# First block of an RWKV and two-expert-layer kernel: routing columns in column halves, three small steps on other engines, another written order

## The chip, the cores and the metric

One core of one Trainium2 chip runs the whole program in one launch. The metric is the device time in microseconds of that core, the median of several runs. The kernel before takes 879.41 us (median of 3 runs, 879.02 to 879.43).

## The reference, cut to what matters

```python
# stage 1: attention with decay, B=4, H=8, S=768, D=48
for t in range(S):
    y[:, :, t] = r_t @ (state + (u * k_t) v_t^T)
    state = w_t * state + k_t v_t^T
x = y as rows [3072, 384]
# stage 2: gated layer, d_ff = 1536
xn = x / sqrt(mean(x * x) + 1e-6) * rms_g
x = (silu(xn @ w_gate) * (xn @ w_val)) @ w_out
# stage 3: 8 experts, top 1, d_ff = 1024
logits = x @ moe2_w_gate ; e = argmax ; gate_w = softmax(logits)[e]
out[rows of e] = gate_w * sigmoid(x @ w_output_gate[:, e]) * (relu(x @ w1[e]) @ w2[e])
```

The logits and the output gate of stage 3 need x only through two small matrices of 384 x 8 each. The kernel folds them into stage 2: the rows of w_out are lengthened from 384 to 400 columns by w_out times those 16 columns. These 16 are the routing columns.

## The kernel before, in words

Stage 2 handles the 3072 rows in 8 blocks of 384 (j = 0 to 7). Within a block, f runs over the 12 parts of d_ff, 128 each. For every f, l1 multiplies x by the gate and value weights (18 matmuls of L170, three for each product: high by high, high by low, low by high), ScalarE takes the silu and VectorE the product h (L546 in the first block). Two f later, l2 adds h times the 400 columns into three accumulators (L560 in the first block). While block j goes through l1 and l2, the attention of the three 128-row tiles of block j+1 is laid between them.

Attention of a tile is a generator (attention, L350 to L501) with nine pieces, each ended by a yield: a scan for kq (L370); the decay and kq product, and k times r on GpSimd (L383, L385); a second scan and rq (L390, L393); a transpose of kq on TensorE (L414), the four small products that give the gains g (L420), g out of PSUM (L424) and the bonus, v times g, on GpSimd (L404); the scores (L437) and their mask on VectorE (L441); the sum with v (L456), y on VectorE (L460), its square on ScalarE (L464), and on GpSimd the mean (L465) and the power -1/2 (L466); the state (L472, L482); the scaling of y (L486); the transposes of y (L490) and x as a high and a low part (xh L494, xl L497). Tiles 0 to 5 are "bare": their g comes from TensorE as told; later tiles take it from another load.

The weights of stage 2 arrive in HBM as 64-bit floats and are decoded on the chip while the first block runs: 18 parts, of which 12 are gate and value weights and 6 are pairs of w_out rows. A part (decode, L101 to L136) goes through five stages: load; low word on ScalarE (L116) and shift on VectorE (L117); merge on VectorE (L121) and sum on GpSimd (L125); high part on ScalarE (L133); low part on VectorE (L135). A step of decoding (decode_step, L772) takes one stage or two of each of several parts; l1 and l2 call it at every second slot. When a pair of w_out rows is decoded, route_columns makes the routing columns of each of its two parts f: three transposes (L512), one copy to SBUF (L515), three matmuls of 128 columns of weights by 16 (L519), and one copy into the lengthened rows (L520).

Everything is in one written order (a manual schedule): each engine takes its instructions in the order in which the program issues them. Before the first l1 that order is START_SEQ: 0, 1 and 2 advance the attention of that tile by one piece, 9 is one decode_step, a negative number -n is n matmuls on constants that feed nothing (warm, L344), and 99 is columns_of (L201), which turns u and rms_g. In the first block OFFS and TGAP say at which slot each piece of tiles 3 to 5 comes. A slot is one call from l1 or l2, 36 in the block.

```python
for d in START: ...            # 99, -n, 9, or a tile
def slot():
    plan.step()
    if plan.slot % 2:
        decode_step()
```

Of the kernel before, what the change touches and what calls it, by code (L numbers as in the profile page):

```python
# [22 lines left out]
def kernel(  # L23
# [15 lines left out]
    ROUTE_AT=(0, 3),  # L39
    OFFS=((0, 0, 6.7, 7.5, 8.8, 10.5, 11.4, 11.5, 12.7), (0, 1.6, 3.2, 4.8, 6.4, 8, 9.6, 11.6, 13.8)),  # L40
    TGAP=(8.9, 9.0),
    START_SEQ=(-11, 0, 0, 0, -4, -4, -6, -1, 99, 0, 1, 0, 1, -4, 9, 0, 1, 1, 2, -4, 0, 0, 1, 9, 2, 0, 1, -4, 2, -6, 1, 9, 2, 1, 2, -4, 1, 2, 9, -2, 2, 2, 9, -6, 2, 9),
):
# [307 lines left out]
    def attention(c, i, xh, xl, col):  # L351
# [31 lines left out]
        nc.vector.tensor_tensor(out=kq, in0=kT, in1=kq, op=ALU.mult)  # L383
        if bare:
            nc.gpsimd.tensor_tensor(out=kT, in0=kT, in1=rT, op=ALU.mult)  # L385
        yield
# [5 lines left out]
        )  # L392
        nc.vector.tensor_tensor(out=rq, in0=rT, in1=rq, op=ALU.mult)  # L393
        if i != NSET and not bare:
            load_tile(i + NSET + (i < NSET))
# [15 lines left out]
        if not last:  # L411
# [4 lines left out]
            nc.scalar.activation(out=kt, in_=kt_ps, func=AF.Copy)  # L416
        if bare:
            g_ps = bank("m", 3, [P, H])
            for p in range(NPR):
                nc.tensor.matmul(  # L420
                    g_ps[:, 2 * p:2 * p + 2], kT[0:64 + D, p], c["u2"][0:64 + D, p], start=True,
                    stop=True,
                )
            nc.scalar.activation(out=g, in_=g_ps, func=AF.Copy)  # L424
            bonus()
            if i != NSET:
                load_tile(i + NSET + (i < NSET))
        if ch:
# [10 lines left out]
        for q in range(2):  # L439
            m = p2.tile([P, NPR, P], F32, tag="am", name="am")  # L440
            nc.vector.tensor_tensor(  # L441
                out=m, in0=ab[q], in1=c["tri"].unsqueeze(1).to_broadcast([P, NPR, P]), op=ALU.mult
            )
            am.append(m)
        yield
        yp = bank("m", 3, [P, H, D])
# [60 lines left out]

    def route_columns(f, tf):

        o = bank("m", 3, [P, KD, P])  # L510
        for kk in range(KD):
            nc.tensor.transpose(o[:, kk], tf[:, kk * P:(kk + 1) * P], c["ident"])  # L512

        wt = p3.tile([P, DM], F32, tag="hl", name="wt").rearrange("p (c f) -> p c f", c=KD)
        nc.scalar.activation(out=wt, in_=o, func=AF.Copy)  # L515
        yield
        o = bank("m", 3, [P, 2 * E])
        for kk in range(KD):
            nc.tensor.matmul(o, wt[:, kk], c["wr"][:, kk], start=kk == 0, stop=kk == KD - 1)  # L519
        nc.scalar.activation(out=whole_w[f // 2][:, f % 2, DM:WIDTH], in_=o, func=AF.Copy)  # L520
        yield

    def split_wo(k):

        for f in (2 * k, 2 * k + 1):
            if f in routed:
                exhaust(routed.pop(f))
        wo[k] = ring.tile([P, 2, 2, WIDTH], FR, tag="big", bufs=6, name="wo")
# [147 lines left out]
    with tc.manual_schedule():  # L676
# [34 lines left out]
        for f in range(KF):  # L711
# [8 lines left out]
            if f % 2:  # L720
# [7 lines left out]

                def more(tf, f=f):
                    for i in range(2):  # L730
                        routed[f - 1 + i] = route_columns(f - 1 + i, tf[:, i])

# [9 lines left out]
        def routed_step():  # L742

            n = done_w[0]
            for f in sorted(routed):
                if f not in plan_r:
                    plan_r[f] = {n + f % 2, n + f % 2 + 2}
                if n in plan_r[f] and next(routed[f], 1):
                    del routed[f]
            for f in [f for f in routed if max(plan_r[f]) < n]:  # L750
                exhaust(routed.pop(f))

# [107 lines left out]
        for j in range(NB):  # L860
# [8 lines left out]
            if j + 1 < NB:  # L869
                nxs = new_x(j + 1)  # L870
                for a in range(sizes[j + 1]):
                    plan.add(
                        attention(c, starts[j + 1] + a, nxs[0], nxs[1], a * P),
                        a * TGAP[j > 0], OFFS[j > 0],
                    )

            def slot():
                plan.step()

                if plan.slot % 2:  # L880
                    decode_step()
# [3 lines left out]
            for f in range(KF + 2):  # L885
# [453 lines left out]
```

## Time and profile before

| | |
|---|---|
| median of 3 runs | 879.41 us |
| the profiled execution | 878.36 us |
| its span, first to last instruction | 876.7 us |
| mean granted TensorE clock | 0.976 |
| TensorE busy | 850.6 us (97%) |
| VectorE busy | 516.8 us (59%) |
| ScalarE busy | 310.0 us (35%) |
| GpSimd busy | 210.4 us (24%) |
| first matmul of l1 in the first block | 47.43 us |
| end of the first block | about 145.9 us |

The profile comes from one execution, whose own time is 1.66 us more than its span and 1.05 us less than the median. Times in a row are microseconds from the start of the span. PE is TensorE, PEld its weight loads, DVE VectorE, ACT ScalarE, POOL GpSimd. A clock of 1.00 is 2.4 GHz, 0.50 is 1.2 GHz. The profile counts two records for each matmul of fp32 operands, so x6 for L519 are three matmuls.

### The profile page before, as it was taken

What the parts mean: (1) busy time and instruction counts of PE and PEld (TensorE: products, weight loads), DVE (VectorE), ACT (ScalarE), POOL (GpSimd) and SP (SyncE); (2) the same over time, 40 slices, a digit from 0 to 9 for tenths busy, and PEclk for the clock granted to TensorE, in tenths of its full rate; (3) what the DMA queues carried; (4) which work ended last, traced back from release to release, by engine and by line L of the source; (5) the groups of instructions that cost most, each with busy time, mean ns of one, the idle gap of its engine ahead of it and who ended that gap; (6) DMA issues with size and microseconds to landing.
All of it is one profiled execution on the core that took longest, in us unless ns stands there. A gap on an engine that the chain in (4) does not pass through costs nothing. (4 is left out here: it accounts for less than half of the span.)

```text
span 876.7 us, 15834 instructions
## 1 busy us (share of the span) xinstructions
PE 850.6 (97%) x6175; PEld 798.5 (91%) x6175; DVE 516.8 (59%) x1027; ACT 310.0 (35%) x653; POOL 210.4 (24%) x282
## 2 busy tenths in 40 slices
PE   7889999999999999999999999999999999999995
PEld 5677878999999999999999999999999999999994
DVE  7788946763764565565376366343646565565641
ACT  4455334322223222322322223223435434443430
POOL 6555522222321122032132132010021022122111
PEclk8669999999999999999999999999999999999998
DMA  8654421762222222131023020012255444435510
GB/s 234 200 166 133 138 89 48 192 186 81 83 55 55 65 65 64 30 99 55 10 88 81 24 82 19 2 40 82 71 184 159 141 157 148 153 121 177 175 42 23
DMA packets 63728, 87.98 MB, mean 100 GB/s; under 512 B 5538, under 2 KB 55220, under 8 KB 63652
## 3 DMA queue, kind: packets, MB, share of 16 engines
q1 hardware_dynamic: 60014, 77.36, 30.1%
q0 software_dynamic: 3312, 9.56, 2.9%
q8 instruction: 49, 0.80, 0.4%
q14 instruction: 27, 0.22, 0.1%
q10 hardware_dynamic: 326, 0.03, 0.0%
HBM read 70.71 MB, written 16.58 MB: 100 GB/s over the span
## 5 line engine op out<-in xcount | busy, mean ns | idle before, releaser
L170 PE MATMUL a<-xh,gv 128*128 128x384 f32 x1152 | 324.7, 347 | 1.6 <-ACT xh L494 1.6
L170 PEld LDWEIGHTS a<-xh,gv 128*128 128x128 f32 x1152 | 212.7, 190 | 5.3 <-ACT xh L494 1.7
L170 PE MATMUL a<-xl,gv 128*128 128x384 f32 x576 | 195.3, 339 | 0.2 <-DVE xl L497 0.2
L170 PEld LDWEIGHTS a<-xl,gv 128*128 128x128 f32 x576 | 109.5, 190 | 1.2 <-DVE xl L497 0.6
L549 DVE TENSOR_TENSOR sil<-a,sil 128x384 f32<-128x384 f32 x84 | 46.7, 555 | 107.1 <-PE a L170 106.0
L542 ACT ACTIVATE sil<-a 128x384 f32<-128x384 f32 x96 | 47.1, 491 | 175.5 <-PE a L170 170.1
L170 PE MATMUL a<-xh,w1s 128*128 128x272 f32 (+7 forms) x384 | 106.1, 337 | 0.4 <-DVE hl L1003 0.4
L551 ACT ACTIVATE hh<-sil 128x384 fp32r<-128x384 f32 x84 | 44.1, 524 | 144.1 <-DVE sil L549 142.4
L571 PE MATMUL l<-wo,hh 128*128 128x400 f32 x252 | 88.5, 351 | 0.0
L572 PE MATMUL l<-wo,hh 128*128 128x400 f32 x252 | 86.5, 343 | 0.0
L573 PE MATMUL l<-wo,hl 128*128 128x400 f32 x252 | 86.2, 342 | 0.0
L246 POOL DMA_INDIRECT out_dram<-row,iu x30 | 35.4, 1179 | 189.3 <-DVE row L1014 146.2
L1003 DVE SCALAR_TENSOR_TENSOR hl<-a,hh 128x256 fp32r<-128x256 f32 (+8 forms) x72 | 38.6, 539 | 68.3 <-ACT hh L1002 68.3
L170 PEld LDWEIGHTS a<-xh,w1s 128*128 128x128 f32 x384 | 69.8, 188 | 2.0 <-DVE hl L1003 0.7
L1002 ACT ACTIVATE hh<-a 128x256 fp32r<-128x256 f32 (+8 forms) x72 | 34.5, 479 | 93.9 <-PE a L170 93.3
L170 PE MATMUL l<-hh,rows 128*128 128x272 f32 (+4 forms) x240 | 67.5, 346 | 0.0
L554 DVE TENSOR_TENSOR hl<-sil,hh 128x384 fp32r<-128x384 f32 x84 | 46.7, 556 | 31.9 <-ACT hh L551 31.9
L170 PE MATMUL a<-xl,w1s 128*128 128x272 f32 (+7 forms) x192 | 64.5, 336 | 0.1
L404 POOL TENSOR_TENSOR y<-vt,g 128x384 f32<-128x384 f32 x23 | 21.0, 914 | 167.0 <-issue 67.9
L571 PEld LDWEIGHTS l<-wo,hh 128*128 128x128 f32 x252 | 47.2, 187 | 1.0
L572 PEld LDWEIGHTS l<-wo,hh 128*128 128x128 f32 x252 | 47.4, 188 | 0.0
L573 PEld LDWEIGHTS l<-wo,hl 128*128 128x128 f32 x252 | 47.2, 187 | 0.0
(250 smaller groups left out, 1453.3 us busy)
## 6 DMA issues: line engine op xcount, KB each, us to landing
raw<-in_moe_w_dram SPq DMA_DIRECT2D x64, 384.0 KB, 3.3
set<-in_feat_dram SPq DMA_DIRECT2D x46, 192.0 KB, 3.6
rk<-in_rkv_dram SPq DMA_DIRECT2D x18, 384.0 KB, 4.1
scr<-zrow SPq DMA_DIRECT2D x8, 788.0 KB, 6.2
set<-in_feat_dram SPq DMA_DIRECT2D x46, 96.0 KB, 2.5
vt<-in_rkv_dram SPq DMA_DIRECT2D x23, 192.0 KB, 2.8
raw<-in_moe_w_gate_dram SPq DMA_DIRECT2D x8, 384.0 KB, 4.6
raw<-in_moe_w_val_dram SPq DMA_DIRECT2D x8, 384.0 KB, 4.0
```

The costliest lines, as they stand in the source:

```text
L170: nc.tensor.matmul(o, a, b, start=start and i == 0, stop=stop and i == 2, skip_group_check=True)
L246: ins = nc.gpsimd.indirect_dma_start(out=dst, out_offset=bass.IndirectOffsetOnAxis(ap=idx, axis=0), in_=rows, in_offset=None, bounds_check ...
L404: nc.gpsimd.tensor_tensor(out=y, in0=vv, in1=g.unsqueeze(2).to_broadcast([P, H, D]), op=ALU.mult)
L542: nc.scalar.activation(out=sil, in_=o, func=AF.Silu)
L549: nc.vector.tensor_tensor(out=sil, in0=pg[1], in1=sil, op=ALU.mult)
L551: nc.scalar.activation(out=hh, in_=sil, func=AF.Copy)
L554: nc.vector.tensor_tensor(out=hl, in0=sil, in1=hh.bitcast(F32), op=ALU.subtract)
L571: nc.tensor.matmul(o, hh[:, sl], wh, start=f == 0, stop=False)
L572: nc.tensor.matmul(o, hh[:, sl], wl, start=False, stop=False)
L573: nc.tensor.matmul(o, hl[:, sl], wh, start=False, stop=f == KF - 1)
L1002: nc.scalar.activation(out=hh, in_=o, func=AF.Relu)
L1003: nc.vector.scalar_tensor_tensor(out=hl, in0=o, scalar=0.0, in1=hh.bitcast(F32), op0=ALU.max, op1=ALU.subtract)
```

## The change

It touches the first 146 us alone, but for one instruction of each attention tile.

- Routing columns: one generator for a pair of w_out rows instead of one for each part. Its two transposes and copies are as before; the products come as 12 matmuls of 64 columns of weights, two halves for each of 3 chunks of 2 parts, and one copy takes both parts into the lengthened rows.
- k times r of tiles 0, 2, 3, 4 and 5 moves from GpSimd to VectorE, behind rq. Tile 1 stays on GpSimd.
- For tiles 2 to 5 the gains (L420 before, L437 now) are issued behind the scores rather than ahead of them.
- The bonus of tiles 1 to 5 moves from GpSimd (one instruction of 128x384) to ScalarE (eight of 128x48, each scaled by its column of g). Tile 0 stays.
- The mean plus 1e-6 (L465 before) moves to ScalarE, for all 24 tiles.
- decode_step: the merge and sum of part n first, then the high part of n - 1, the low part of n - 2, and the load of n + 2 last. Before: load, shift, low part of n - 2, merge and sum, high part.
- START_SEQ and the slots of tiles 3 to 5 (OFF0, a list for each tile) are others.

```diff
-    OFFS=((0, 0, 6.7, 7.5, 8.8, 10.5, 11.4, 11.5, 12.7), (0, 1.6, 3.2, ...)),
-    TGAP=(8.9, 9.0),
-    START_SEQ=(-11, 0, 0, 0, -4, -4, -6, -1, 99, 0, 1, 0, 1, -4, 9, 0, 1, 1, 2, ...),
+    ROUTE_STEP=3,
+    KT_DVE=(0, 2, 3, 4, 5),
+    BONUS_ACT=(1, 2, 3, 4, 5),
+    SS_ACT=True,
+    G_LATE=(2, 3, 4, 5),
+    DEC=((0, 3), (-1, 4), (-2, 5), (2, 1), (0, 2)),
+    OFF0=((0, 1.5, 6.7, ...), (9.4, 9.4, 15.6, ...), (17.8, 19.3, 24.0, ...)),
+    START_SEQ=(-11, 0, 0, -4, 0, -1, 99, -6, -6, -8, 1, 0, 1, 0, 0, 0, -4, 1, 9, ...),
...
-        if bare:
-            nc.gpsimd.tensor_tensor(out=kT, in0=kT, in1=rT, op=ALU.mult)
+        kt_mul = nc.vector if i in KT_DVE else nc.gpsimd
+        if bare and i not in KT_DVE:
+            kt_mul.tensor_tensor(out=kT, in0=kT, in1=rT, op=ALU.mult)
...
         nc.vector.tensor_tensor(out=rq, in0=rT, in1=rq, op=ALU.mult)
+        if bare and i in KT_DVE:
+            kt_mul.tensor_tensor(out=kT, in0=kT, in1=rT, op=ALU.mult)
...
         def bonus():
+            if i in BONUS_ACT:
+                for h in range(H):
+                    nc.scalar.activation(
+                        out=y[:, h], in_=vv[:, h], func=AF.Copy, scale=g[:, h:h + 1]
+                    )
+                return
...
-        nc.gpsimd.tensor_scalar(ss, ss, 1.0 / DM, 1e-6, op0=ALU.mult, op1=ALU.add)
+        if SS_ACT:
+            nc.scalar.activation(out=ss, in_=ss, func=AF.Copy, scale=1.0 / DM, bias=1e-6)
...
+        o = bank("m", 3, [P, 2, 2 * E])
+        for i in range(2):
+            for kk in range(KD):
+                for t in (slice(0, 64), slice(64, P)):
+                    nc.tensor.matmul(
+                        o[t, i], wt[i][:, kk, t], c["wr"][:, kk], start=kk == 0,
+                        stop=kk == KD - 1, skip_group_check=True,
+                    )
+        nc.scalar.activation(out=whole_w[k][:, :, DM:WIDTH], in_=o, func=AF.Copy)
...
-                advance(n + 2, 1)
-                advance(n, 2)
-                if n >= LAG:
-                    advance(n - LAG, 5)
-                advance(n, 3)
-                if n >= LAG - 1:
-                    advance(n - LAG + 1, 4)
+                for d, stage in DEC:
+                    if n + d >= 0:
+                        advance(n + d, stage)
```

What the written order does on the engines stands here at three places; the rows give the order alone. On VectorE, from tile 0's rq (set_80) to tile 2's first scan (kq<-rv). Before:

```order
L393 TENSOR_TENSOR rq<-set_80,rq 128x4x128
L370 SCALAR_TENSOR_TENSOR kq<-set_81,back 128x516
L441 TENSOR_TENSOR am<-m,tri 128x512 x2
L382 RECIPROCAL front<-kq 128x4
L383 TENSOR_TENSOR kq<-set_81,kq 128x4x128
L117 TENSOR_SCALAR dt<-raw_144 128x768
L121 SCALAR_TENSOR_TENSOR dt<-raw_144,dt 128x768
L460 TENSOR_TENSOR y<-m,y 128x384
L390 SCALAR_TENSOR_TENSOR rq<-set_81,front 128x516
L393 TENSOR_TENSOR rq<-set_81,rq 128x4x128
L370 SCALAR_TENSOR_TENSOR kq<-rv,back 128x516
```

Now:

```order
L402 TENSOR_TENSOR rq<-set_80,rq 128x4x128
L404 TENSOR_TENSOR set_80<-set_80 128x512
L378 SCALAR_TENSOR_TENSOR kq<-set_81,back 128x516
L390 RECIPROCAL front<-kq 128x4
L391 TENSOR_TENSOR kq<-set_81,kq 128x4x128
L461 TENSOR_TENSOR am<-m,tri 128x512 x2
L482 TENSOR_TENSOR y<-m,y 128x384
L399 SCALAR_TENSOR_TENSOR rq<-set_81,front 128x516
L402 TENSOR_TENSOR rq<-set_81,rq 128x4x128
L125 TENSOR_SCALAR dt<-raw_144 128x768
L129 SCALAR_TENSOR_TENSOR dt<-raw_144,dt 128x768
L378 SCALAR_TENSOR_TENSOR kq<-rv,back 128x516
```

k times r of tile 0 has come in, tile 1's kq stands ahead of tile 0's mask, and the two steps on the first weight part stand behind tile 0's y and tile 1's rq.

On ScalarE, from tile 2's y (whose square is am,ss<-y) to its xh, the last thing that the first l1 waits for. Before:

```order
L464 ACTIVATE am,ss<-y 128x384
L116 ACTIVATE rv<-rv 128x768
L515 ACTIVATE wt<-m 128x384
L482 ACTIVATE states<-m 48x4x48 x2
L486 ACTIVATE y<-y,ss 128x384
L116 ACTIVATE raw_405<-raw_405 128x768
L133 ACTIVATE gv<-dt 128x768
L515 ACTIVATE wt<-m 128x384
L494 ACTIVATE xh<-m,g_col 128x128 x3
```

Now:

```order
L486 ACTIVATE am,ss<-y 128x384
L488 ACTIVATE ss<-ss 128x1
L519 ACTIVATE xh<-m,g_col 128x128 x3
L507 ACTIVATE states<-m 48x4x48 x2
L511 ACTIVATE y<-y,ss 128x384
L124 ACTIVATE raw_427<-raw_427 128x768
L141 ACTIVATE gv<-dt 128x768
L541 ACTIVATE wt<-m 128x384
L519 ACTIVATE xh<-m,g_col 128x128 x3
```

The mean has come in behind the square, tile 1's xh stands here, and the low word and one copy of the routing columns have gone ahead of the square; the three steps ahead of tile 2's xh are of the same kind as before.

On TensorE, in tile 2 (its set is rv), from its transposes to its sum with v. Before (the matmuls on constants between the scores and the next transposes left out):

```order
L414 MATMUL m<-ident,kq 128x128 x4
L420 MATMUL m<-u_86,rv 128x2 x4
L437 MATMUL m<-rq,kq 128x128 x8
...
L490 MATMUL m<-ident,y 128x128 x3
L456 MATMUL m<-rv,am 64x48 x16
```

Now (four matmuls on constants behind the first row, two ahead of the last):

```order
L431 MATMUL m<-ident,kq 128x128 x4
...
L457 MATMUL m<-rq,kq 128x128 x8
L437 MATMUL m<-u_86,rv 128x2 x4
L539 MATMUL m<-ident,rv 128x128 x3
...
L478 MATMUL m<-rv,am 64x48 x16
```

The scores have gone ahead of the gains, tile 1's transposes of y (L490) no longer stand ahead of tile 2's sum, and a routing transpose (L539, of the first w_out pair) stands there.

## Rows read from the trace of the kernel before

**Rows 1.** Page, busy time of each engine, share of the span, instructions.
```profile
PE 850.6 (97%) x6175; PEld 798.5 (91%) x6175; DVE 516.8 (59%) x1027; ACT 310.0 (35%) x653; POOL 210.4 (24%) x282
```
**Rows 2.** Stretches: length, busy us of each engine, granted clock, DMA share, GB/s.
```profile
0.00:47.40 47.40, 37.16 (x307) 25.59 (x307) 35.95 (x47) 23.58 (x49) 28.67 (x37) 0.77 0.72 202
47.40:59.50 12.10, 10.39 (x34) 9.88 (x35) 11.41 (x15) 5.19 (x10) 6.58 (x4) 0.50 0.61 207
59.50:145.90 86.40, 83.81 (x622) 69.40 (x621) 63.06 (x91) 38.49 (x81) 33.64 (x39) 1.00 0.37 113
145.90:870.00 724.10, 719.26 (x5216) 693.68 (x5214) 406.38 (x876) 242.74 (x514) 141.56 (x205) 1.00 0.30 91
```
**Rows 3.** Waits of TensorE, 47.4 to 146 us: total, times, longest.
```profile
PE m L512 <- POOL rv L125: 2.1, 2, 1.5
...
PE m L490 <- ACT y L486: 1.1, 1, 1.1
PE m L512 <- POOL wlast L125: 0.8, 1, 0.8
```
**Rows 4.** Timeline of VectorE, start and length in us, idle time before in brackets.
```profile
8.65 1.23 DVE L390 TENSOR_TENSOR_SCAN rq<-set,front 128x516 f32<-128x516 f32 x1
...
16.20 0.56 DVE L117 TENSOR_SCALAR dt<-raw 128x768 uint32<-128x768 uint32 x1
...
18.62 0.55 DVE L460 TENSOR_TENSOR y<-m,y 128x384 f32<-128x384 f32 x1
19.09 2.68 DVE L390 TENSOR_TENSOR_SCAN rq<-set,front 128x516 f32<-128x516 f32 x1
...
27.48 0.66 DVE L383 TENSOR_TENSOR kq<-rv,kq 128x512 f32<-128x512 f32 x1
...
36.60 1.29 DVE L441 TENSOR_TENSOR am<-m,tri 128x512 f32<-128x512 f32 x2 [1.86 <-PE m L437]
...
40.75 0.55 DVE L460 TENSOR_TENSOR y<-m,y 128x384 f32<-128x384 f32 x1
...
82.45 0.94 DVE L135 TENSOR_TENSOR gv<-dt,gv 128x768 fp32r<-128x768 f32 x1
```
**Rows 5.** Timeline of TensorE, tile 2 and the first l1.
```profile
35.19 1.78 PE L437 MATMUL m<-rq,kq 48*128 48x128 f32 x14 [1.25 <-ACT rv L416]
...
47.43 0.69 PE L170 MATMUL a<-xh,gv 128*128 128x384 f32 x1 [1.60 <-ACT xh L494]
...
53.82 0.90 PE L512 MATMUL m<-ident,rv 128*128 128x128 f32 x3 [1.47 <-POOL rv L125]
```
**Rows 6.** Timeline of ScalarE and GpSimd around tile 2's y.
```profile
44.04 0.61 ACT L486 ACTIVATE y<-y,ss 128x384 f32<-128x384 f32 x1 [0.37 <-POOL ss L466]
...
47.01 0.88 ACT L494 ACTIVATE xh<-m,g_col 128x128 fp32r<-128x128 f32 x3
...
18.83 1.84 POOL L125 TENSOR_TENSOR dt<-dt,raw 128x768 int32<-128x768 int32 x1 [0.95 <-DVE dt L121]
...
42.03 0.65 POOL L465 TENSOR_SCALAR ss<-ss 128x1 f32<-128x1 f32 x1 [4.54 <-ACT am L464]
```
**Rows 7.** Timeline of TensorE, routing products and 64-column products at full clock.
```profile
63.38 0.74 PE L519 MATMUL m<-wr,wt 128*128 128x16 f32 x6
63.96 0.42 PE L170 MATMUL a<-xh,gv 128*128 128x384 f32 x1
...
77.91 0.34 PE L170 MATMUL a<-xl,gv 128*128 128x384 f32 x1
78.08 0.34 PE L170 MATMUL a<-xh,gv 128*128 128x384 f32 x1
78.35 1.14 PE L456 MATMUL m<-vt,am 128*64 128x48 f32 x32
79.42 0.84 PE L519 MATMUL m<-wr,wt 128*128 128x16 f32 x6
80.11 0.42 PE L170 MATMUL a<-xh,gv 128*128 128x384 f32 x1
```

More of the change, by code (lines that the diff above doesn't have):

```diff
@@ L416, in attention, with gains @@
             nc.scalar.activation(out=kt, in_=kt_ps, func=AF.Copy)
-        if bare:
+        def gains():
             g_ps = bank("m", 3, [P, H])
@@ L427, in attention @@
                 load_tile(i + NSET + (i < NSET))
+        if bare and i not in G_LATE:
+            gains()
         if ch:
@@ L444, in attention @@
             am.append(m)
+        if bare and i in G_LATE:
+            gains()
         yield
@@ L464, in attention @@
         nc.scalar.activation(out=sq, in_=y2, func=AF.Square, accum_out=ss)
-        nc.gpsimd.tensor_scalar(ss, ss, 1.0 / DM, 1e-6, op0=ALU.mult, op1=ALU.add)
+        if SS_ACT:
+            nc.scalar.activation(out=ss, in_=ss, func=AF.Copy, scale=1.0 / DM, bias=1e-6)
+        else:
+            nc.gpsimd.tensor_scalar(ss, ss, 1.0 / DM, 1e-6, op0=ALU.mult, op1=ALU.add)
         nc.gpsimd.tensor_tensor(out=ss, in0=ss, in1=c["mhalf"], op=ALU.pow)
@@ L506, with route_columns @@
     routed = {}
[L508 to L520, printed above, removed]
+    def route_columns(k, tf):
+        wt = []
+        for i in range(2):
+            o = bank("m", 3, [P, KD, P])
+            for kk in range(KD):
+                nc.tensor.transpose(o[:, kk], tf[:, i, kk * P:(kk + 1) * P], c["ident"])
+            t = p3.tile([P, DM], F32, tag="hl", name="wt").rearrange("p (c f) -> p c f", c=KD)
+            nc.scalar.activation(out=t, in_=o, func=AF.Copy)
+            wt.append(t)
+            yield
+        o = bank("m", 3, [P, 2, 2 * E])
+        for i in range(2):
+            for kk in range(KD):
+                for t in (slice(0, 64), slice(64, P)):
[4 more added lines that the diff above has]
+        nc.scalar.activation(out=whole_w[k][:, :, DM:WIDTH], in_=o, func=AF.Copy)
         yield
     def split_wo(k):
-        for f in (2 * k, 2 * k + 1):
-            if f in routed:
-                exhaust(routed.pop(f))
+        if k in routed:
+            exhaust(routed.pop(k))
         wo[k] = ring.tile([P, 2, 2, WIDTH], FR, tag="big", bufs=6, name="wo")
@@ L727, in whole, with more @@
                     return whole_w[k][:, :, 0:DM]
-                def more(tf, f=f):
-                    for i in range(2):
-                        routed[f - 1 + i] = route_columns(f - 1 + i, tf[:, i])
+                def more(tf, k=f // 2):
+                    routed[k] = route_columns(k, tf)
                 pieces.append(([
@@ L744, in routed_step @@
             n = done_w[0]
[L745 to L751, printed above, removed]
+            for k in sorted(routed):
+                if k not in plan_r:
+                    plan_r[k] = {n, n + 1, n + ROUTE_STEP}
+                if n in plan_r[k]:
+                    next(routed[k], None)
+            for k in [k for k in routed if max(plan_r[k]) <= n]:
+                exhaust(routed.pop(k))
         spare = [ring_view([2, DM, 2], U32, False) for _ in range(2)]
@@ L873 @@
                         attention(c, starts[j + 1] + a, nxs[0], nxs[1], a * P),
-                        a * TGAP[j > 0], OFFS[j > 0],
+                        a * TGAP if j else 0, OFFS if j else OFF0[a],
                     )
@@ L878, in slot @@
                 plan.step()
-                if plan.slot % 2:
+                if plan.slot % DSLOT[1] in DSLOT[:1] if j == 0 else plan.slot % 2:
                     decode_step()
@@ L890 @@
                 if f >= 2:
-                    if f - 2 in routed:
-                        exhaust(routed.pop(f - 2))
+                    if (f - 2) // 2 in routed:
+                        exhaust(routed.pop((f - 2) // 2))
                     if j == 0:
```

7 lines of the change are left out of this document (5 added, 2 removed).

## The prediction

> **What bounds the kernel now.** I read the page's busy times first, then the span cut into stretches, then the waits of TensorE in the first block, then the timelines of the start. The page says that TensorE is busy 97% of the span [rows 1]; the stretches say where the other 3% lie [rows 2]. From 145.9 to 870 us, seven blocks and the experts, TensorE works 719.3 of 724.1 us, and the other 4.8 hold the last output behind its last matmul. That part cannot shrink unless TensorE gets less work, and the change gives it the same. So a microsecond won or lost before 145.9 us arrives at the end in full, and the forecast is about the first 146 us. They fall in three pieces. Up to 47.4 us TensorE waits for the attention of tiles 0 to 2; its 37.2 busy us there include matmuls on constants, so busy says nothing. From 47.4 to 59.5 us it runs l1 at a clock of 0.50, 1.2 GHz. From 59.5 to 145.9 us it runs at 1.00, 2.4 GHz, and is busy 83.8 of 86.4 us. VectorE is busy 36.0 of the first 47.4 us and 63.1 of the 86.4; it is second, with room.
>
> **Start.** The first l1 begins at 47.43 because tile 2's xh ends there: TensorE waits 1.60 us for it [rows 5]. Back from there: xh at 47.01, scaling of y at 44.04 [rows 6], y at 40.75, mask at 36.60 [rows 4], scores at 35.19 after 1.25 us of waiting for a copy on ScalarE [rows 5]. Ahead of those, VectorE's own queue sets the pace: two decode steps stand from 16.20 to 18.62 ahead of tile 0's y, and tile 1's second scan takes 2.68 us where the same scan took 1.23 at 8.65 [rows 4]; beside the long one ran a sum on GpSimd from 18.83 to 20.67 [rows 6].
>
> What the change does there, edit by edit:
> - *Order on VectorE.* Tile 0's y comes when TensorE has the sum ready, not behind 2.4 us of decoding. With the same product times, but k times r of tile 0 ahead, I get y of tile 0 at about 16.8 in place of 18.62, 1.8 us earlier.
> - *k times r on VectorE* for tiles 0 and 2: 2 x 0.66 us by the product of the same shape [rows 4], inside this chain; GpSimd gives up its two, so less runs beside VectorE. I put this at zero net: 1.3 us in, and of one stretch like the 1.45 us above (2.68 - 1.23) about as much out.
> - *Scores ahead of gains* for tile 2: the 1.25 us wait goes, since the second bank of the scores no longer is the one that ScalarE has still to copy. This is the clearest single gain on the chain.
> - *Mean on ScalarE*: 0.65 us on GpSimd [rows 6] becomes a one-column instruction right behind the square, where no engine is changed; 0.5 us off the chain.
> - *Bonus on ScalarE* for tiles 1 and 2: no row shows 128x48 there. Nearest is xh, three of 128x128 in 0.88 us, 0.29 each [rows 6]; eight of these at most 2.3 us for each tile, and nothing if they fall into ScalarE's waits. ScalarE is busy 23.6 of 47.4 us [rows 2], but tile 1's bonus stands ahead of the scaling of tile 0's y, so of two I charge half of one, 1.2 us at most, and take 0.5.
> - *Tile 2's sum with v* no longer stands behind tile 1's transposes on TensorE. Behind it is now tile 1's xl; a whole decode step stands ahead of tile 2's y on VectorE, under TensorE's sum. I count nothing.
> - *Three ScalarE steps ahead of xh* stay three; the matmuls on constants fill waits. Zero, unless they are late (a rival below).
>
> Sum: 1.8 + 1.25 + 0.5 - 0.5 = 3.05, and what follows from it: tile 1's second scan ends about 3.3 us earlier (1.8, and 1.45 of stretch that its new place avoids, since the first sum on GpSimd now comes behind it). Following the chain through both tiles with every VectorE step at its unstretched length gives 6.0 us; with one stretch of 1 to 1.5 us at each of the three sums on GpSimd that now fall beside VectorE's chain, it gives 3.4. I take **4.5 us**, between. The lower end for the range is 1.8, tile 0's y alone; the upper 6.0.
>
> **Routing products.** Before: three matmuls of a part take 63.96 - 63.38 = 0.58 us of TensorE, 1.16 for a pair [rows 7]. Now 24 records of 64 columns. The sum with v is 32 such records in 79.42 - 78.35 = 1.07 us, 0.033 each, so 0.80. Coming to 64 columns from 128 costs 78.35 - 78.08 = 0.27 in place of 0.17 us, and leaving them 80.11 - 79.42 = 0.69 in place of 0.58 [rows 7], 0.2 together. So 1.0 against 1.16, about 0.2 for each of six pairs at full clock and more at half: **1.2 us**. Ends: nothing, and 2.2 (no cost of change, 6 x 0.36). The six copies saved on ScalarE lie beside other work. The Trainium skill speaks against this edit: "TensorEngine Tiling (Array Packing)", section Key Properties, says that a change of tiling mode drains TensorE, and each pair now has two such changes. By that rule the edit would bring about nothing; the sum would be 1.2 us less. The rows above show a change, at 0.1 us each.
>
> **First stretch of l1.** 12.1 us at 1.2 GHz, with a 1.47 us wait at 53.82 for the sum on GpSimd of the second w_out pair, which stands ahead of the first part's second half on TensorE [rows 5, 2]; full clock came 5.7 us after that wait, at 59.5. The merge and sum of a part now come ahead of a low part in each step, so this sum is ready, by the chain above, about 4.5 us after l1 begins, when TensorE gets there. I take 1.2 of the 1.47, and 0.3 because full clock comes a little earlier: **1.5 us**. Lower end: minus 3, if the wait stays and the clock returns 6 us later (half of it lost). Upper: 4.
>
> **The rest of the first block.** TensorE waits there for GpSimd sums in front of routing transposes (2.1 - 1.5 = 0.6, and 0.8) and 1.1 for a scaling of y [rows 3]. A low part took 0.94 us ahead of the merge in the same step [rows 4]; now it stands behind, so the two waits for sums go: **1.4 us**. The 1.1 stays. k times r adds 3 x 0.66 = 2.0 us to VectorE's 63.1 of 86.4, and three GpSimd products leave; the bonus adds up to 6.9 us to ScalarE's 38.5 of 86.4. Both lie beside TensorE's work; without that cover the first is 2.0 us. Ends: minus 2, plus 2.6.
>
> **Sum.** 4.5 + 1.2 + 1.5 + 1.4 = 8.6 us off the profiled execution's 878.36: 869.8. The median stands 1.05 above that execution, so **870.8 us**, 1.0% less.
>
> **Rivals.** 0.2%, 1.76 us, is about what a measurement can tell from no change.
> - *The start is not won* (0.13). x would be ready earlier, but the weights not: loads and sums keep their pace, and TensorE waits in front of routing transposes instead of for xh. For it: at 53.82 it did wait for a sum. Against: VectorE has idle time in the start, and each load follows a sum that comes earlier too. It gives the forecast without 4.5: 875.3.
> - *The halves bring nothing* (0.10), by the drain. If every change made TensorE finish what it has, 0.17 us of overlap between two l1 matmuls and about 0.19 at the end of the 64-column records would go, 0.36 for a pair: 0.80 + 0.36 = 1.16, as before. 872.0.
> - *The matmuls on constants delay tile 0* (0.06): twenty now stand between columns_of and tile 0's transposes. If u arrives late, tile 0 is 2 us later and the 1.8 is gone: 872.6.
> - *Slower: 1.2 GHz through a large part of the block* (0.06). Place: the routing transposes of each pair, ahead of l1's matmuls in TensorE's queue. If TensorE waits there at the first four pairs for a sum, as it did at 53.82, the full clock does not come. Every busy us at half clock costs half of one. The point of decision: 17 us more at half clock than before eat the 8.6. With 25 us more it is 870.8 + 12.5 = 883.3. Against: waits of 0.6 to 1.1 us after 59.5 left the clock at 1.00 [rows 2, 3].
>
> **How the numbers follow.** The forecast, all four terms within their nearer bounds, has 0.65 and spans 867 to 873.5. The next three rivals lie between 872 and 875.3, still under 877.65, the line for "faster"; of the first I leave a quarter above it, for a block that also loses a little (0.03 each to same and slower). The range reaches from 866.5, the start's upper end with all else, to 877, which leaves out the slow rival and the tails. Faster 0.86, same 0.05, slower 0.09.
>
> **What would show it.** In the changed profile: first l1 matmul near 43 us (right: 41.4 to 45.6; wrong: over 46); no wait of 1.25 us at tile 2's scores; routing products at 1.0 us for a pair at full clock (1.16 or more is wrong); full clock before 55 us; waits for GpSimd sums in the block under 0.5 us together; the first block's end near 137. A time of 870 with l1 still at 47 us would mean that the reasons are wrong, and so would a gain that comes behind 146 us.

## The result, and the profile after

The changed kernel takes 868.09 us (median of 4 runs, 867.46 to 869.49), the kernel before beside it 879.21 (4 runs, 876.79 to 879.43): a ratio of 0.988, 95% interval 0.986 to 0.990. The forecast was 870.8 in a range of 866.5 to 877. The profiled execution took 868.61 us with a span of 866.9, against 878.36 and 876.7.

The page, busy time of each engine [rows 1], and the stretches [rows 2] of the changed kernel. The line numbers are now, on TensorE, L178 for l1, L437 the gains, L457 the scores, L478 the sum with v, L515 the transposes of y, L539 the routing transposes and L548 the routing products; on ScalarE L519 is xh, on GpSimd L133 a decoding sum.

```profile
PE 841.2 (97%) x6249; PEld 789.6 (91%) x6249; DVE 513.1 (59%) x1032; ACT 324.2 (37%) x711; POOL 192.2 (22%) x248
```

```profile
43.10:48.85 5.75, 5.12 (x36) 4.19 (x37) 5.21 (x7) 4.68 (x8) 3.29 (x2) 0.59 0.45 137
48.85:133.42 84.57, 82.75 (x695) 68.55 (x694) 66.06 (x98) 43.95 (x102) 29.42 (x20) 1.00 0.39 119
137.00:860.00 723.00, 717.58 (x5203) 691.79 (x5201) 407.33 (x875) 245.56 (x530) 136.47 (x185) 1.00 0.31 91
```

The first two stretches are the first block: from the first l1 to the point at which its matmuls are seen to run at 2.4 GHz, and from there to the first of the three copies of the block's result out of PSUM (L963, L937 before; the 145.9 us in the table of the kernel before are the third copy, which now starts at 134.8). The same two of the kernel before:

```profile
47.43:59.55 12.12, 10.44 (x35) 9.93 (x35) 11.46 (x15) 5.16 (x10) 6.60 (x4) 0.51 0.61 206
59.55:144.59 85.04, 82.45 (x617) 68.62 (x617) 62.18 (x87) 37.48 (x79) 32.48 (x28) 1.00 0.36 109
```

The start is 4.33 us shorter (43.10 in place of 47.43), the block 6.84 (90.32 in place of 97.16). From its end to the last matmul 1.34 us are given back (722.43 in place of 721.09), which leaves 9.83. The granted clock of the first stretch is 0.59 and not 0.50: the clock was back before l1's matmuls show it, under the routing products, at about 47.8 us (in the kernel before at about 59.4):

```profile
43.10:47.79 4.69, 4.47 (x27) 3.64 (x29) 4.16 (x7) 4.08 (x7) 2.59 (x2) 0.50 0.54 166
47.79:48.85 1.06, 0.65 (x15) 0.56 (x13) 1.06 (x1) 0.60 (x2) 0.70 (x1) 1.00 0.02 9
```

So the block can be divided into three parts: TensorE's idle time, half of its busy time at 1.2 GHz (what the low clock costs), and the rest, its work counted at 2.4 GHz. Before: idle (12.12 - 10.44) + (85.04 - 82.45) = 4.27, low clock 5.16, work 87.7. After: idle 2.45, low clock 4.47 / 2 = 2.23, work 85.6. So of 6.84 us, 1.82 are waiting, about 2.9 clock and 2.1 work. The split is no finer than half a microsecond: the same kernel in another execution (below) has 85.0 of work.

TensorE's timeline of the changed kernel, tile 2 to the first stretch of l1 (start and length in us, idle time before in brackets) [rows 5]:

```profile
30.38 1.16 PE L457 MATMUL m<-rq,kq 48*128 48x128 f32 x16
31.83 1.05 PE L437 MATMUL m<-u,rv 112*128 112x2 f32 x8 [0.29 <-ACT rv L433]
...
35.26 1.95 PE L478 MATMUL m<-rv,am 128*64 128x48 f32 x32
...
43.10 0.69 PE L178 MATMUL a<-xh,gv 128*128 128x384 f32 x1 [0.93 <-ACT xh L519]
...
48.55 0.55 PE L539 MATMUL m<-ident,rv 128*128 128x128 f32 x3 [0.41 <-POOL rv L133]
48.85 0.42 PE L178 MATMUL a<-xh,gv 128*128 128x384 f32 x1
...
61.79 0.55 PE L539 MATMUL m<-ident,rv 128*128 128x128 f32 x3 [0.94 <-POOL rv L133]
...
77.50 0.88 PE L548 MATMUL m<-wr,wt 128*64 128x16 f32 x24
78.31 0.55 PE L539 MATMUL m<-ident,rv 128*128 128x128 f32 x3
```

The scores no longer wait. The wait of 1.47 us for the second w_out pair's sum is now 0.41, and the first l1 matmul behind it, at 48.85, takes 0.42 us where the first of all took 0.69. One routing pair takes 78.31 - 77.50 = 0.81 us.

VectorE's timeline, the rows that answer to [rows 4]:

```profile
15.89 0.56 DVE L482 TENSOR_TENSOR y<-m,y 128x384 f32<-128x384 f32 x1 [1.19 <-PE m L478]
16.37 1.22 DVE L399 TENSOR_TENSOR_SCAN rq<-set,front 128x516 f32<-128x516 f32 x1
...
32.10 1.28 DVE L461 TENSOR_TENSOR am<-m,tri 128x512 f32<-128x512 f32 x2
...
37.32 0.56 DVE L482 TENSOR_TENSOR y<-m,y 128x384 f32<-128x384 f32 x1 [1.17 <-PE m L478]
```

Tile 0's y starts at 15.89 instead of 18.62, tile 1's second scan is 1.22 us long instead of 2.68, tile 2's mask starts 4.50 us earlier and its y 3.43. On ScalarE [rows 6] the scaling of tile 2's y and its xh:

```profile
40.10 0.61 ACT L511 ACTIVATE y<-y,ss 128x384 f32<-128x384 f32 x1
...
42.69 0.88 ACT L519 ACTIVATE xh<-m,g_col 128x128 fp32r<-128x128 f32 x3
```

### The profile page after: what moved, and what is told of

Its sections match the earlier page's. It is cut to its first block, busy times and chain, and to the rows that moved or that the text cites. A ratio compares the mean times of both kernels' runs of the same rounds, so it can differ in the third digit from the quotient of the medians.

```text
span 866.9 us, 15973 instructions
## 1 busy us (share of the span) xinstructions
PE 841.2 (97%) x6249; PEld 789.6 (91%) x6249; DVE 513.1 (59%) x1032; ACT 324.2 (37%) x711; POOL 192.2 (22%) x248
## 5 line engine op out<-in xcount | busy, mean ns | idle before, releaser
L178 PE MATMUL a<-xh,gv 128*128 128x384 f32 x1152 | 321.8, 345 | 1.3 <-ACT xh L519 0.9
L178 PEld LDWEIGHTS a<-xh,gv 128*128 128x128 f32 x1152 | 211.0, 188 | 5.9 <-ACT xh L519 1.6
L178 PE MATMUL a<-xl,gv 128*128 128x384 f32 x576 | 194.3, 337 | 0.2 <-DVE xl L522 0.2
L178 PEld LDWEIGHTS a<-xl,gv 128*128 128x128 f32 x576 | 108.7, 189 | 1.1 <-DVE xl L522 0.6
L178 PE MATMUL a<-xh,w1s 128*128 128x272 f32 (+7 forms) x384 | 106.2, 337 | 0.4 <-DVE hl L1029 0.4
L178 PEld LDWEIGHTS a<-xh,w1s 128*128 128x128 f32 x384 | 69.8, 188 | 2.0 <-DVE hl L1029 0.6
L178 PE MATMUL l<-hh,rows 128*128 128x272 f32 (+4 forms) x240 | 67.5, 346 | 0.0
L178 PE MATMUL a<-xl,w1s 128*128 128x272 f32 (+7 forms) x192 | 64.6, 336 | 0.1
L421 POOL TENSOR_TENSOR y<-vt,g 128x384 f32<-128x384 f32 x19 | 17.3, 912 | 166.5 <-issue 62.9
L491 POOL TENSOR_TENSOR ss<-ss,mhalf 128x1 f32<-128x1 f32 x24 | 14.5, 604 | 151.9 <-ACT ss L488 151.9
L603 PEld LDWEIGHTS l<-wo,hh 128*128 128x128 f32 x252 | 47.4, 188 | 0.4 <-issue 0.3
```

The source lines that it names most:

```text
L178: nc.tensor.matmul(o, a, b, start=start and i == 0, stop=stop and i == 2, skip_group_check=True)
L421: nc.gpsimd.tensor_tensor(out=y, in0=vv, in1=g.unsqueeze(2).to_broadcast([P, H, D]), op=ALU.mult)
L603: nc.tensor.matmul(o, hh[:, sl], wl, start=False, stop=False)
```

## The experiments

All are the changed kernel with one part undone or varied. The kernel before ran beside each: 876.99 us in the first four, 875.67 in the next four, 878.25 in the last four. These medians differ by 2.6 us, so times are compared within a group, and otherwise by the traces. No run undoes the new slots of tiles 3 to 5 (OFF0), so what they bring in the block is not told apart.

**The order of the start undone.**

```diff
-    START_SEQ=(-11, 0, 0, -4, 0, -1, 99, -6, -6, -8, 1, 0, 1, 0, 0, 0, -4, 1, ...),
+    START_SEQ=(-11, 0, 0, 0, -4, -4, -6, -1, 99, 0, 1, 0, 1, -4, 9, 0, 1, 1, ...),
```

> The changed kernel with the old START_SEQ; every other edit stays. My theory: the order at the start is what brings the first l1 forward (43.10 in place of 47.43 us), with the small steps giving about 1 us of it; so here the first l1 comes at 45.5 to 47.5 us and the time is 3 to 5 us over the changed kernel's 868.1. Rival (the small steps on other engines bring it forward, not the order): the first l1 stays under 44.5 us and the time within 1.5 us of 868.1.

872.67 us (870.35 to 872.85), ratio 0.9938 (0.9915 to 0.996); the other three of its group with the new order take 868.71, 868.72 and 871.29. Its timeline of TensorE:

```profile
46.99 0.44 PE L178 MATMUL a<-xh,gv 128*128 128x384 f32 x1 [1.79 <-ACT xh L519]
...
52.82 0.90 PE L539 MATMUL m<-ident,rv 128*128 128x128 f32 x3 [1.63 <-POOL rv L133]
```

The first l1 is back where it was, 3.9 us later than in the changed kernel, while the block from there takes 90.67 us, as short as in the changed kernel. Tile 0's y is at 18.61 again and tile 1's second scan 2.67 us long (18.62 and 2.68 before). So START_SEQ carries the gain in the start, some 4 us, and nothing of the gain in the block; the steps on other engines don't bring the first l1 forward without it (46.99 against 47.43). START_SEQ also holds the matmuls on constants, 58 now and 52 before, and the run undoes both at once: order and constants are not told apart.

**Routing products at full width, still a pair at once.**

```diff
-                for t in (slice(0, 64), slice(64, P)):
-                    nc.tensor.matmul(
-                        o[t, i], wt[i][:, kk, t], c["wr"][:, kk], ...
+                nc.tensor.matmul(
+                    o[:, i], wt[i][:, kk], c["wr"][:, kk], ...
```

> The changed kernel with three matmuls of 128 columns for each part instead of column halves; the pair still shares one bank and one copy. My theory from the changed trace: a pair's products take 0.82 us in halves and 1.17 us at full width, so 5 pairs x 0.35 and some more for the pair at half clock: 1.8 to 2.5 us slower than the changed kernel, about 870.3. The forecast's own size was 1.2 us. Rival (the change of tiling mode drains, halves bring nothing): no slower, 868.1, and a pair at full width under 0.9 us.

868.71 us (868.47 to 869.12), ratio 0.9904 (0.9878 to 0.9929). The 1.8 to 2.5 us that this run was expected to lose don't show: its time does not separate it from the changed kernel, which has no run in this group. The trace does. A pair at full clock, and the two stretches of the block:

```profile
76.06 1.41 PE L547 MATMUL m<-wr,wt 128*128 128x16 f32 x12
77.32 0.53 PE L539 MATMUL m<-ident,rv 128*128 128x128 f32 x3
```

```profile
41.74:47.49 5.75, 5.54 (x25) 5.13 (x25) 5.22 (x7) 4.72 (x8) 3.23 (x2) 0.59 0.58 180
47.49:133.45 85.96, 84.59 (x635) 71.78 (x634) 66.05 (x98) 43.92 (x104) 29.37 (x20) 1.00 0.38 118
```

A pair takes 77.32 - 76.06 = 1.26 us in place of 0.81. Counted as above (the clock was back at 46.4 us here), the work in the block is 87.9 us, close to the 87.7 of before; in the changed kernel and all variants with halves it was 84.6 to 85.7. So nearly all of the work saved is the halves' doing, 2.1 us or more, and the pairing alone saves no work that shows. In length the block loses less: 91.71 us here against 90.32 and 90.56 in the two executions of the changed kernel.

**The old order of a decode step.**

```diff
-    DEC=((0, 3), (-1, 4), (-2, 5), (2, 1), (0, 2)),
+    DEC=((2, 1), (0, 2), (-2, 5), (0, 3), (-1, 4)),
```

> The changed kernel with the old order inside a decoding step (load, shift, low part, merge and sum, high part). My theory: each low part (0.95 us on VectorE) stands ahead of the sum again, so the waits of TensorE for sums in front of the routing transposes grow from 1.3 us together to 2.5 us or more, and the full clock comes later: 1 to 3 us slower than 868.1. Rival (the order inside the step hides behind the 8 to 13 us by which parts are ready ahead of their l1): within 0.7 us of 868.1.

868.72 us (867.71 to 869.84), ratio 0.9901 (0.9873 to 0.9929). TensorE's waits of 40 to 140 us, total, times, longest:

```profile
PE m L539 <- POOL rv L133: 1.7, 1, 1.7
```

Its row in the timeline:

```profile
48.40 0.55 PE L539 MATMUL m<-ident,rv 128*128 128x128 f32 x3 [1.67 <-POOL rv L133]
```

The wait for the second pair's sum is 1.67 us again, and the matmuls, at 2.4 GHz at 48.70, are back at 1.2 GHz from 49.4 to 52.8. The block takes 92.12 us, 1.6 to 1.8 more than in the two executions of the changed kernel. The decode order does what was forecast, in the trace; in time it is under what can be told.

**All four small steps undone** (k times r, bonus, mean, gains).

```diff
-    KT_DVE=(0, 2, 3, 4, 5),
-    BONUS_ACT=(1, 2, 3, 4, 5),
-    SS_ACT=True,
-    G_LATE=(2, 3, 4, 5),
+    KT_DVE=(),
+    BONUS_ACT=(),
+    SS_ACT=False,
+    G_LATE=(),
```

> The changed kernel with k times r, the bonus and the mean back on GpSimd and the gains ahead of the scores; both sequences, the halves and the decoding order stay. My theory: GpSimd's steps stand in the start's chain again, and tile 2's scores wait again: the first l1 1 to 3 us later than 43.10, and longer VectorE steps beside GpSimd in the block; 2 to 5 us slower than 868.1. Rival (they are covered, the order does it all): within 1 us of 868.1.

871.29 us (870.93 to 871.95), ratio 0.9935 (0.9916 to 0.9955). The first l1 is at 43.66, half a microsecond later; the block takes 92.46 us, with more waits for sums:

```profile
PE m L539 <- POOL rv L133: 2.4, 4, 1.1
...
PE m L539 <- POOL wlast L133: 0.5, 1, 0.5
```

Together the four are worth 2.6 us beside the two runs above, each of which has another part undone. Where it lies is not settled: beside the traces of the changed kernel it is the block that is longer, by about 2 us, but beside those two runs the first l1 is 1.7 to 1.9 us later and the block 0.3 to 0.8 longer. The next runs take the four one by one.

**The changed kernel again.** No edit; it stands beside the next three.

> The changed kernel once more, unaltered, as the measure for the runs beside it. Two runs with the same start had their first l1 at 41.7 and 42.0 us where the changed kernel's profile had 43.10. My theory: the difference is the granted clock under tile 2's sum with v (1.95 us for it at 1.2 GHz, 1.14 at 2.4 GHz), which differs from run to run; so the first l1 falls between 41.5 and 43.3, and 0.8 us earlier where that sum takes 1.14. Rival: it is fixed by the code, and comes at 43.10 again. Time 866.5 to 869.5 either way.

867.91 us (866.29 to 868.39), ratio 0.9906 (0.9877 to 0.9935). The first l1 starts at 43.00, the block takes 90.56 us. The earlier starts of the two runs above (41.74 and 42.01) did not come back. Its two stretches, and a part of its timelines:

```profile
43.00:53.03 10.03, 9.59 (x49) 8.64 (x50) 8.93 (x13) 5.24 (x9) 5.18 (x3) 0.52 0.52 156
53.03:133.56 80.53, 80.00 (x680) 66.30 (x680) 61.21 (x92) 43.26 (x101) 27.51 (x20) 1.00 0.37 116
```

```profile
43.00 0.69 PE L178 MATMUL a<-xh,gv 128*128 128x384 f32 x1 [1.45 <-ACT xh L519]
...
48.45 0.90 PE L539 MATMUL m<-ident,rv 128*128 128x128 f32 x3 [0.23 <-POOL rv L133]
...
59.18 2.43 POOL L133 TENSOR_TENSOR rv<-rv,raw 128x768 int32<-128x768 int32 x1 [1.55 <-DVE rv L129]
...
61.93 0.55 PE L539 MATMUL m<-ident,rv 128*128 128x128 f32 x3
```

The block is as long as in the first execution, but made up otherwise: idle 0.97, low clock 4.6, work 85.0, where it was 2.45, 2.2 and 85.6. The clock came back at about 52.7 us rather than 47.8, and the waits that the first execution had at 56 to 62 us are not there. The reason shows in GpSimd's row: the next sum ends at 59.18 + 2.43 = 61.61 here and at 61.73 in the first execution (59.30 + 2.43, last section), whatever TensorE's clock. TensorE came to it early in the first execution and waited 0.94 us, and came late here and did not. Between 50 and 62 us VectorE, which feeds these sums, was busy for 11.89 us in the first execution and 10.82 here. The other runs agree: all five executions whose clock was back by 47.8 us wait for h at 54 to 57 us and for this sum at 60 to 63; of the six whose clock was back between 52 and 54 us five have neither wait, and one (small steps undone) has the second. So an early clock is given back as waits for what VectorE and GpSimd still decode, and clock and waits are not two separate gains.

**Gains ahead of the scores again.**

```diff
-    G_LATE=(2, 3, 4, 5),
+    G_LATE=(),
```

> The changed kernel with the gains of tiles 2 to 5 ahead of the scores again. The forecast's theory: tile 2's scores then wait again for the copy of its transposes on ScalarE (1.25 us before) and stand behind the gains (0.9 us), so the first l1 comes 1 to 2 us later and the time is 1 to 2 us more. Rival: tile 2's mask on VectorE stands behind a decoding step that ends at 32.1 us anyway, so up to 1.5 us is hidden and the first l1 moves by under 0.7 us.

870.58 us (868.79 to 872.4), ratio 0.9937 (0.9911 to 0.9963): 2.7 us slower than the repeat beside it. But the first l1 starts at 42.52, no later. The loss is in tile 4, in the block. TensorE, and VectorE beside it:

```profile
85.76 0.38 PE L431 MATMUL m<-ident,kq 128*128 128x128 f32 x2
88.50 1.02 PE L437 MATMUL m<-u,set 112*128 112x2 f32 x8 [2.36 <-issue]
...
91.93 1.44 PE L457 MATMUL m<-rq,kq 48*128 48x128 f32 x10
```

```profile
87.72 0.68 DVE L404 TENSOR_TENSOR set<-set 128x512 f32<-128x512 f32 x1
```

The gains wait 2.36 us and start as k times r (L404) ends at 88.40; the profile names no releaser, the times do. Soon after it l1 runs at 1.2 GHz, from 90.1 to 93.5 us (0.52 us a matmul). The block takes 94.10 us, 3.54 more than in the repeat: 2.0 of idle time and 1.9 of low clock, less 0.3 of work.

**k times r on GpSimd again.**

```diff
-    KT_DVE=(0, 2, 3, 4, 5),
+    KT_DVE=(),
```

> The changed kernel with k times r of tiles 0, 2, 3, 4 and 5 on GpSimd again (1.3 to 2.2 us each in place of 0.69 on VectorE). The forecast's theory: zero net on the chain of the start, so the first l1 stays within 0.7 us and the time within 1 us. Rival: VectorE's steps beside GpSimd's product stretch (2.68 in place of 1.23 us in the kernel before), and the gains of tile 0 wait for it: 1.5 to 3 us slower.

868.18 us (867.78 to 868.83), ratio 0.9917 (0.9889 to 0.9944): the same as the repeat. By the trace it has two sides: the first l1 comes at 41.91, 1.1 us earlier, and the block takes 91.74 us, 1.2 more, with a wait of 1.33 us for h and one of 0.91 for a sum. Zero net, as forecast. Of the 1.1 us, 0.6 go with the clock: tile 2's sum with v takes 1.14 us here, at 2.4 GHz, and 1.76 in the repeat, where the clock fell during it.

**Bonus on GpSimd again.**

```diff
-    BONUS_ACT=(1, 2, 3, 4, 5),
+    BONUS_ACT=(),
```

> The changed kernel with the bonus of tiles 1 to 5 on GpSimd again. In the changed trace the eight ScalarE instructions take 1.92 us for a tile, and tile 1's stand ahead of the scaling of tile 0's y, for which TensorE waits 3.3 us. The forecast's theory: they cost half a microsecond on the chain, so without them the first l1 comes 0.3 to 1 us earlier, and the block is about even: within 1 us of the changed kernel, not slower. Rival: on GpSimd the bonus stands ahead of the sums and of the power, so sums and scaling come later: 1 to 2 us slower.

867.43 us (866.43 to 868.11), ratio 0.9905 (0.9876 to 0.9934), first l1 at 42.84, block 90.30 us. The bonus on ScalarE brings nothing that shows.

**k times r and gains both as before**, with the other edits kept.

```diff
-    KT_DVE=(0, 2, 3, 4, 5),
+    KT_DVE=(),
-    G_LATE=(2, 3, 4, 5),
+    G_LATE=(),
```

> The changed kernel with k times r on GpSimd and the gains ahead of the scores, both as in the kernel before. With gains first alone, tile 4's gains waited 2.4 us in the block, until k times r on VectorE behind rq was done, and the clock fell to 1.2 GHz after it; 870.6 us. My theory: the late gains are needed only because k times r moved behind rq; with k times r on GpSimd, early in the tile, gains ahead of the scores wait for nothing: within 1 us of the changed kernel (867.9 beside it in its last runs). Rival: the place of the gains matters by itself: 870 or more again.

869.63 us (869.11 to 870.55), ratio 0.9911 (0.9889 to 0.9934). The 2.36 us wait of the gains is not there. So the late gains are what the move of k times r calls for: it stands behind rq on VectorE, and gains that come ahead of the scores have to wait for it. Idle time in the block is 4.76 us, as in the run with k times r alone on GpSimd (4.08), and more than in the changed kernel; the time lies between the two theories, and its distance to the changed kernel, which has no run in this group, is not settled.

**Mean on GpSimd again.**

```diff
-    SS_ACT=True,
+    SS_ACT=False,
```

> The changed kernel with the mean on GpSimd again. With all four small steps undone the time was 871.3, with k times r or the bonus alone undone 868.2 and 867.4. My theory (the forecast's): the mean on GpSimd costs about 0.5 us on each tile's chain in the start, where tile 0's and tile 2's scaling are waited for, so 0.5 to 1.5 us slower, first l1 0.5 to 1 us later. Rival: it is hidden, within 0.5 us, and the loss with all four undone comes from the gains alone or from several steps meeting on GpSimd.

869.08 us (868.27 to 869.29), ratio 0.990 (0.9878 to 0.9922). Tile 2's y on VectorE and its scaling on ScalarE, first here, then in the repeat of the changed kernel:

```profile
36.70 0.56 DVE L482 TENSOR_TENSOR y<-m,y 128x384 f32<-128x384 f32 x1 [0.20 <-PE m L478]
40.12 0.62 ACT L511 ACTIVATE y<-y,ss 128x384 f32<-128x384 f32 x1 [0.90 <-POOL ss L491]
```

```profile
37.23 0.56 DVE L482 TENSOR_TENSOR y<-m,y 128x384 f32<-128x384 f32 x1 [0.45 <-PE m L478]
40.01 0.61 ACT L511 ACTIVATE y<-y,ss 128x384 f32<-128x384 f32 x1
```

From y to scaling 3.42 us here, 2.78 there: the mean's place is worth 0.64 us of the chain. But y came 0.53 earlier in this execution, so the first l1 stands at 43.09 against 43.00, and no difference in time can be told.

**More constants under the last wait, decode a little earlier or later.** Two variants of the end of START_SEQ: the first puts six more matmuls on constants ahead of tile 2's transposes and two more behind them, where TensorE waits for tile 2's xh; the second has the six too, and puts both last decode steps behind tile 2.

```diff
-    START_SEQ=(..., 2, 1, 2, 2, 9, 2, 9, -2),
+    START_SEQ=(..., 2, 1, 2, 2, 9, -6, 2, 9, -4),
```

> The changed kernel with six more matmuls on constants ahead of tile 2's transposes, where TensorE waits 1.9 us, and two more behind them, where it waits 0.9 us. My theory: TensorE's waits ahead of l1 put the first matmuls of l1 at 1.2 GHz (0.32 us apart until 48.9 us in one run, 52 us in another); with the waits filled, l1 begins at 2.4 GHz or reaches it 3 us earlier: 1 to 3 us faster than the changed kernel, about 866. Rival: the constants come after the clock has fallen, or delay tile 2's transposes: within 0.5 us, or slower by 0.5.

```diff
-    START_SEQ=(..., 2, 1, 2, 2, 9, 2, 9, -2),
+    START_SEQ=(..., 2, 1, 2, 2, -6, 2, -2, 9, 9),
```

> The changed kernel with tile 2's transposes and xh ahead of the last two decoding steps of the start, and eight matmuls on constants around those transposes. Three ScalarE steps (2.1 us) no longer stand ahead of xh. My theory: the first l1 comes 1.0 to 1.5 us earlier and runs sooner at 2.4 GHz: 1.5 to 4 us faster than the changed kernel. Rival: the two decoding steps come as much later, TensorE waits for the sum of the second w_out pair in front of its transposes by 1.5 to 2.5 us, and nothing is won: 867 to 869.

The first takes 867.39 us (866.96 to 867.78), ratio 0.9883 (0.9861 to 0.9905), the second 870.82 (868.78 to 871.14), 0.9923 (0.9901 to 0.9944). The first has the earliest block end of all runs (132.04) and is 0.5 and 0.7 us under the changed kernel's two medians, which are from other groups and whose ranges it overlaps: that it is faster is not shown. TensorE in the first, then in the second:

```profile
41.77 0.44 PE L178 MATMUL a<-xh,gv 128*128 128x384 f32 x1 [1.11 <-ACT xh L519]
...
42.95 0.77 PE L178 MATMUL a<-xh,gv 128*128 128x384 f32 x2
43.52 0.53 PE L178 MATMUL a<-xl,gv 128*128 128x384 f32 x1
```

```profile
40.89 0.44 PE L178 MATMUL a<-xh,gv 128*128 128x384 f32 x1
...
49.30 0.90 PE L539 MATMUL m<-ident,rv 128*128 128x128 f32 x3 [5.04 <-POOL rv L133]
49.86 0.67 PE L178 MATMUL a<-xh,gv 128*128 128x384 f32 x1
```

The second shows what the rival "the start is not won" describes: x is ready 2.2 us earlier than in the changed kernel, l1 begins at 2.4 GHz, and TensorE then waits 5.04 us for the sum of the next pair and runs at 1.2 GHz to 53.8. It is not quite that rival, since this edit also moves the decoding: the sum ends at 49.25 in place of 48.50. But 0.75 us of a wait of 5.04 is all that this explains; the rest is TensorE being there earlier. In this start, x that is ready earlier than the decoded weights wins nothing.

## Why the prediction was right, point by point

- **Start, 4.5 us: measured 4.33.** The mechanism is the one forecast: tile 0's y no longer behind two decode steps (2.73 us earlier, 1.8 forecast), and the next scan unstretched (1.22 in place of 2.68 us). The run with the old START_SEQ takes both away. That the sum comes so near is in part luck: its first four items came out at 2.73, nothing, 0.64 and nothing lost, where 1.8, 1.25, 0.5 and 0.5 lost were forecast; the 4.5 was a choice between 3.4 and 6.0; and among runs with the new order the first l1 lay between 41.7 and 43.7 us.
- *Mean, 0.5 won:* 0.64 in the chain. *Bonus, 0.5 lost:* not there; the eight took 1.92 us a tile, under the bound of 2.3, and with the bonus back on GpSimd the first l1 came at 42.84 against 43.00. *k times r, zero net:* right, though by 1.1 us in the start, part of it clock, against 1.2 in the block.
- **The step that failed** is "scores ahead of gains", put as "the clearest single gain on the chain" with 1.25 us: with the gains first again the first l1 came at 42.52, no later. In that run the mask of tile 2 does start later (33.23; 32.10 in the changed kernel, 32.72 in its repeat), but y does not (36.77; 37.32 and 37.23). Between them stands a join that the order rows of the change show and that the forecast did not price: ahead of tile 2's sum with v TensorE waits in front of a routing transpose for GpSimd's sum, here in the changed kernel, then with the gains first:

```profile
33.93 0.76 PE L539 MATMUL m<-ident,rv 128*128 128x128 f32 x3 [1.04 <-POOL rv L133]
```

```profile
34.35 0.55 PE L539 MATMUL m<-ident,rv 128*128 128x128 f32 x3 [0.95 <-POOL rv L133]
...
35.15 1.14 PE L478 MATMUL m<-rv,am 128*64 128x48 f32 x32
```

In the repeat this transpose starts at 34.55, so the place of the gains does not set it. The clock helped the run with the gains first: its sum with v took 1.14 us, against 1.95 in the changed kernel and 1.76 in the repeat, so that its y and its first l1 came half a microsecond earlier. The edit earns its place in tile 4, where the forecast had put nothing.
- **Routing, 1.2 us: measured about 2.1** for the six pairs, (1.16 - 0.81) x 6, and 2.1 for all work of TensorE in the block (2.7 in the repeat). In the block's length it is 1.2 to 1.4 (91.71 us at full width), and in the time it can't be told. The mis-sized term is the 0.2 us of change into and out of the halves; besides, the forecast's own rows give 0.16 us a pair, which it rounded up to 0.2. A whole pair, changes included, takes 0.81 us, the bare 24 x 0.033. The Trainium skill, "TensorEngine Tiling (Array Packing)", Key Properties, speaks of a drain at each change of mode; here no time for one shows beside the 0.81, and the rival built on it (872.0, halves worth nothing) falls by the run at full width, 1.26 us a pair. That rival's 0.19 us at the end of the halves stands in no row; in the changed kernel the halves' record ends 0.07 us behind the start of the next row (77.50 + 0.88 against 78.31).
- **First stretch, 1.5 us, and waits in the block, 1.4.** Together 2.9: 2.6 of waits and 0.3 of clock. Measured 4.7 in the first execution (waits 1.82, clock 2.9) and 3.8 in the repeat (3.30 and 0.5). The wait at the second pair fell from 1.47 to 0.41 and 0.23, as forecast (1.2 of 1.47); the run with the old decode order brings it back (1.67), and so does the run with the old START_SEQ (1.63), so it takes both. One term put at nothing was wrong: "the 1.1 stays", a scaling of y for which the kernel before waits in the block:

```profile
110.89 0.55 PE L490 MATMUL m<-ident,y 128*128 128x128 f32 x3 [1.10 <-ACT y L486]
```

It is gone from the changed kernel and its repeat. It does not come back with the old START_SEQ, at full width or with the small steps undone; with the old decode order there is one of 0.58. Which edit removed it is open, the slots of tiles 3 to 5 being the one that no run undoes. The forecast treated clock and waits as separate; the repeat shows that they trade. Its sign of rightness "full clock before 55 us" held (47.8 and 52.7), the block's end "near 137" came at 134.8 by the same mark, and "waits for GpSimd sums under 0.5 us together" held in the repeat (0.23) and not in the first execution (0.41 + 0.94).
- **Behind the block** the forecast had a microsecond arrive in full. The first execution gave 1.34 back between block end and last matmul. The repeat took 721.36 us there, near the 721.09 of before, and the other runs 721.2 to 722.3. The only part of the change that reaches there is the mean on ScalarE, and the two runs with the mean on GpSimd are no shorter (722.10 and 722.33). So it is a spread between executions; its cause is open.
- **Sum.** 8.6 forecast for the profiled execution, 878.36 - 868.61 = 9.75 measured (the medians differ by 11.1): 0.2 less in the start, 2.7 more in the block, 1.3 given back.
- **The rivals.** *Start not won:* no, but the last run shows how near it lies. *The halves bring nothing:* no, as told above. *Constants late for tile 0:* its transposes started at 10.72 instead of 8.79, yet its gains at 11.26 instead of 10.99, since before they waited 1.54 us for k times r on GpSimd. No 2 us went. *1.2 GHz through the block:* from 47.8 us in the changed kernel and from 52.7 in its repeat the clock stood at 1.00.

## What to carry to other kernels

Price a move of work to another engine together with the place it takes in that engine's queue: here the written start was worth 4 us, while the single moves of k times r and of the bonus were worth nothing that shows, and the first of them costs 2.7 us where its consumer, the gains, is not moved behind it. Before a wait is booked as a gain, follow the chain past it to the next join and look whether anything there is already waiting on another input. When two gains draw on the same supplier (here the clock's return and the waits for decoded weights), add them once, not twice.

## What was not expected of the hardware

- **When the clock returns varies between executions of one kernel.** From the first l1 to its first matmul at 2.4 GHz: 5.75 us in one, 10.03 in the other. In the first the granted clock fell to 0.50 at about 41.0 us, right behind TensorE's 1.94 us wait for tile 2's scaled y, and rose at 47.8; in the repeat it fell at about 42.4, within the 1.45 us wait for xh, and rose at 52.7. Over the ten runs with the new START_SEQ whose l1 began at 1.2 GHz, the return went with the wait for xh: after a wait of 0.77 to 0.93 us l1 was at full clock 5.8 us behind its start (6.7 in the run with the old decode order, where it was lost again), after 1.14 to 1.45 us 8.4 to 10.2 us behind it. No run changed that wait alone, so this is a correlation and no cause.
- **A clock at 2.4 GHz can go right after work begins.** With eight more constants l1 began at 0.44 us a matmul, behind a wait of 1.11 us for xh, and was at 0.53 within 2 us of its start: the granted clock fell to 0.50 at about 43.0 us.
- **The power on GpSimd** (128x1) took 0.55 us for tile 2 where it took 1.24 before, and sums of decoding 1.84 to 2.65 us, from one to the next. VectorE's scan of 128x516 still takes 2.40 us where such a sum runs beside it, in place of 1.22:

```profile
59.30 2.43 POOL L133 TENSOR_TENSOR rv<-rv,raw 128x768 int32<-128x768 int32 x1 [1.54 <-DVE rv L129]
```

```profile
60.42 2.40 DVE L399 TENSOR_TENSOR_SCAN rq<-set,front 128x516 f32<-128x516 f32 x1
```
